# GpSimd stops scaling queries in batch 4, and its residual adds are laid out apart from VectorE's two-input operations

## The chip, the cores and the metric

The kernel runs on one core of one Trainium2 chip. The metric is the device time of one execution in microseconds. The median of three runs of the kernel before is 551.96 us (551.89 to 552.12).

## The reference

The input is attention data of 8 batches, 12 heads, 448 positions and a head dimension of 64, a mixing pair U, V of rank 32, and two channel matrices of 768 x 3072 and 3072 x 768. Cut to what matters:

```python
q_n = q / (norm(q) + 1e-6);  k_n = k / (norm(k) + 1e-6)
attn = softmax(q_n @ k_n.T / tau)            # per batch and head
x = (attn @ v), heads side by side           # 8 x 448 x 768
u = x + (x.T @ U @ V).T                      # mixes along the positions
out = u + relu(u @ w_ch1) @ w_ch2            # 8 x 448 x 768, float32
```

So each query and key is divided by its length, attention follows, then a low-rank mixing along the sequence with a residual, then a two-layer channel network with a residual.

## The kernel before, in words

**Tiling.** The 12 heads of a batch are 6 pairs. Queries and keys are loaded by GpSimd's DMA queue (L588), four heads at a time, as tiles of 112 partitions (`qk_all`). For each such group `squares` makes the squares (L636 on ScalarE, L640 on VectorE, L638 on GpSimd in one group of batch 0), L644 on VectorE sums them by head, L658 and L659 on ScalarE take the root by a logarithm and an exponential, and L664 and L666 on VectorE make the inverse. Then `norm` multiplies queries and keys by it, one operation of 112 x 512 elements for a pair of heads (L712): these are the unit vectors. SyncE's queue transposes each pair's unit vectors with a DMA (L728) into `sqk`. TensorE makes the scores in bursts of three tiles (L774, six or eight matmuls), ScalarE takes their exponential (L792), TensorE multiplies by the values (L819, 32 matmuls for a pair of heads), and VectorE divides by the row sums (L850 and L851), which also frees the PSUM banks of that product. The mixing is done by L934 (with U), a copy (L1439 on ScalarE or L1441 on VectorE), L987 (with V) and the residual add L996. The result goes through device memory (L1025) and comes back transposed (L884) and plain (L888).

**The channel network.** It runs over the 28 tiles of 128 rows: three tiles, one tile, and then 12 units of two tiles. A unit uses seven block products where plain blocking uses eight. In the first six of these units, the half-way units, only the second layer is done so: the first layer is L1263 with its relu in L1273 (ScalarE) or L1275 (VectorE), the sums of blocks that the seven products need are L1235, L1236, L1237 and L1246 on VectorE, and the products are L1292. ScalarE copies the first product out of PSUM (L1315), GpSimd makes three residual adds from that copy and the rows of u (L1317, 128 x 384 elements of float32 each, both inputs in SBUF), and VectorE adds the further products to them (L1310). The other six units do the first layer by seven products as well (L1156 on TensorE, L1178, L1184 and L1193 beside it), after sums of the weights (L1115 to L1118). `mlp_seven` makes both kinds; its argument `up` is None in a half-way unit.

**What sets the order.** Every operation is entered in a `Plan` with an engine, an assumed duration, what it depends on, the ring slots that it takes and frees, and a priority. `Plan.run` walks through assumed time and writes the instructions of each engine in the order in which it started them; on the chip each engine follows its order and waits on semaphores. TensorE and GpSimd have streams that keep their own order; VectorE, ScalarE and SyncE choose by priority among what is ready. An operation entered with `port=True` on VectorE isn't started in the plan while one of GpSimd's with `port=True` runs, and the reverse:

```python
def shared(o, e, r):
    return max(r, port["POOL" if e == "DVE" else "DVE"]) if o.port and e in port else r
```

On VectorE that holds for L640, L712, L1235 to L1237, L1246 and the sums of weights and columns. On GpSimd it holds for L638 and for L712. The chip has no such rule from the plan: there only the order and the semaphores count. While attention of the later batches goes on, the half-way units fill TensorE between bursts of scores and value products, all in one order.

`POOL_XN` gives, by batch, which of queries (0) and keys (1) have their L712 on GpSimd. Before the change that is batch 4's queries: six instructions, one for each pair.

Of the kernel before, what the change touches and what calls it, by code (L numbers as in the profile page):

```python
# [317 lines left out]
def kernel(  # L318
# [21 lines left out]
    CH = C // 2  # L340
# [7 lines left out]
    BURST = [1] + [2] + [3] * 6  # L348
    PLAIN = [3, 1]
    HALF = 6  # L350
    POOL_XN = {4: (0,)}
    WHOLE = 3
    LAST = {0: 0, 2: 2, 4: 4}
    WIDE = 1
# [155 lines left out]
    pool_y = plan.stream("POOL")  # L510
# [11 lines left out]
    def dve_t(n, fast=1, fixed=0.065):  # L522
        return fixed + n * 0.00105 / fast
# [176 lines left out]
    def norm(b, p, ld, la, inv, a, deps, pr, loaded):  # L700
# [6 lines left out]
        def part(i):  # L707
            def fn():
# [3 lines left out]
                (nc.gpsimd if pool_ else nc.vector).tensor_mul(dst, src, sc)  # L712
            pool_ = i in POOL_XN.get(b, ())
            return plan.add(Op("POOL" if pool_ else "DVE", 1.05 if pool_ else dve_t(512), fn, deps=[deps[i]], acq=[xn],
# [383 lines left out]
    def seven_rows(after, free):  # L1098

        A_ = w1_sb.rearrange("p (i e) (j g x) -> p i e j g x", e=2, g=2, x=128)  # L1100
        N = HF * 128
        homes = [X_t[:, 0:N], X_t[:, N:2 * N], qk_t[:, 1152:1152 + N],
                 v0[:, 0:N], qk_t[:, 3 * QC + 1024:3 * QC + 1024 + N], v0[:, N:2 * N]] + [
            attn_all[:, N * n:N * (n + 1)] for n in range(3)]
        homes = [x.rearrange("p (j x) -> p j x", x=128) for x in homes]
        S1, S2, S4 = homes[0:3], homes[3:6], homes[6:9]
        by = {}

        def rows_(f, deps, prio=2.5, eng="DVE"):
            e = nc.gpsimd if eng == "POOL" else nc.vector  # L1110
            return plan.add(Op(eng, N * 0.00203 if eng == "POOL" else 0.15 + N * 0.00053, lambda: f(e), deps=deps, prio=prio,
                               port=True), pool_s if eng == "POOL" else None)
        for i in (2, 0, 1):
            A11, A12, A21, A22 = A_[:, i, 0, :, 0], A_[:, i, 1, :, 0], A_[:, i, 0, :, 1], A_[:, i, 1, :, 1]
            a = rows_(lambda v, o=S1[i], x=A21, y=A22: v.tensor_add(o, x, y), free[i])  # L1115
            c = rows_(lambda v, o=S2[i], x=S1[i], y=A11: v.tensor_sub(o, x, y), [a, *free[3 + i]])
            d = rows_(lambda v, o=S4[i], x=A12, y=S2[i]: v.tensor_sub(o, x, y), [c, *free[6]], 3, "POOL" if i in () else "DVE")
            e = rows_(lambda v, o=A21, x=A11, y=A21: v.tensor_sub(o, x, y), [a, *after], 2.7)  # L1118
            by[i] = {3: d, 5: a, 6: c, 7: e}
        left = {1: lambda i, j: A_[:, i, 0, j, 0], 2: lambda i, j: A_[:, i, 1, j, 0], 3: lambda i, j: S4[i][:, j],  # L1120
                4: lambda i, j: A_[:, i, 1, j, 1], 5: lambda i, j: S1[i][:, j], 6: lambda i, j: S2[i][:, j],
                7: lambda i, j: A_[:, i, 0, j, 1]}
        return left, by
# [127 lines left out]
    def mlp_seven(tiles, right, made_by, up=None, after=()):  # L1251
# [4 lines left out]
        if up is None:  # L1256
            us, uT, ut = columns_of(tiles)
            rs = {}
            for j in range(HF):
                mm = Slot(r_up, 1)  # L1260
                for e in range(2):
                    for cc in range(CC):
                        o = plan.add(Op("PE", pe_t(256), lambda j=j, e=e, cc=cc, mm=mm: nc.tensor.matmul(  # L1263
                            out=mm.tile[:, 256 * e:256 * e + 256], lhsT=w1_sb[:, cc, (2 * j + e) * 128:(2 * j + e + 1) * 128],
                            rhs=uT.tile[:, cc, :], start=(cc == 0), stop=(cc == CC - 1)),
                            deps=ut if cc == 0 else [], acq=[mm] if cc == 0 and e == 0 else [], rel=[uT.slot]), pe_mlp)
# [36 lines left out]
        s1, y12, y22, y21, o11 = Slot(r_o, 3), *[Slot(r_o, 0) for _ in range(4)]  # L1303
# [8 lines left out]
        def tile_of(s):  # L1312
            return lambda: s.tile
        p1 = product(1, a, True, False)
        cp = plan.add(Op("ACT", 0.42, lambda: nc.scalar.copy(out=s1.tile, in_=a.tile[:, 0:CH]),  # L1315
                         deps=[p1, *after], acq=[s1], prio=-0.5))
        y = [plan.add(Op("POOL", 1.0, lambda y_=y_, u=u, c0=c0: nc.gpsimd.tensor_add(  # L1317
            out=y_.tile, in0=s1.tile, in1=u.tile[:, c0:c0 + CH]), deps=[cp, u.back], acq=[y_], rel=[s1, u]), pool_y)
            for y_, u, c0 in ((y12, u1, CH), (y22, u2, CH), (y21, u2, 0))]
        if up is not None:  # L1320
            d = Slot(r_mm4, 1)
# [188 lines left out]
    def att(b):  # L1510
# [17 lines left out]
        out=lead.tile[:, i], in_=src[0, 0:2].rearrange("h (s c) d -> s h (c d)", c=SC)),  # L1528
        acq=[uv], prio=-5, lat=2.5)) for i, src in enumerate((q, k))]
# [8 lines left out]
    for c in range(SC):  # L1538
# [8 lines left out]
                        deps=[zf, *begun], prio=-2, lat=12.0))]  # L1547
# [45 lines left out]
    for n in range(0, len(rest), 2):  # L1593
        if n // 2 == HALF:
            up = seven_rows([hosts[-1][0][-1]], [
                [o for t in range(4) for o in made[3, t][:1]]] * 2 + [
                [o for p in range(NPAIR) for o in got[B - 1, p, "qkT"][1]] if i in (2, 4) else
                [last_av[B - 1 if i == 6 else B - 2, p] for p in range(NPAIR)] for i in range(2, 7)])
            held = stores + [last_av[B - 1, p] for p in range(NPAIR)]
            up = *up, [o for p in range(NPAIR) for o in got[B - 1, p, "qkT"][1]], [last_av[B - 1, p] for p in range(NPAIR)], bursts[B - 1][-1:]  # L1600
        hosts.append(mlp_seven(rest[n:n + 2], *seven, *((up, held) if n // 2 >= HALF else ())))
# [52 lines left out]
```

## Time and profile before

| | |
|---|---|
| median of the runs | 551.96 us |
| profiled execution | 551.44 us |
| its span, first to last instruction | 549.4 us |
| TensorE, matmuls | 539.7 us busy, 98% |
| VectorE | 447.4 us, 81% |
| ScalarE | 284.8 us, 52% |
| GpSimd | 149.6 us, 27% |
| granted TensorE clock | 1.0 |

GpSimd's busy time holds its DMA issues (some 0.7 us each) as well as its arithmetic. How to read rows of the profile: a row of a timeline gives the start and the duration in us, the engine (PE is TensorE, PEld its weight loads, DVE VectorE, ACT ScalarE, POOL GpSimd), the line, the operation, its output and input by name, and how many instructions are merged; the bracket at the end is idle time before it and what ended that. A row of the waits says who waited for whom: us in total, how often, the longest. A row of groups gives a count, then busy us and mean ns of one, then idle us in front of the group and what ended them. A row of the table by stages gives the stage, its length, and the busy us of PE, PEld, DVE, ACT and POOL with the numbers of instructions, then clock, DMA share and GB/s.

### The profile page before, as it was taken

The page shows a single profiled execution, that of the slowest core. Times are in us where ns is not written, and L with a number is a line of the kernel's source. Part 1 is how long each engine was busy: PE and PEld are TensorE (multiplying, and loading weights), DVE is VectorE, ACT ScalarE, POOL GpSimd, SP SyncE. Part 2 cuts the span into 40 slices and gives each one's busy share as a digit, 9 for nine tenths or more (in the row PEclk, how much of TensorE's full clock was granted, in tenths as well). Part 3 has the DMA queues.
Part 4 walks back from the last instruction along what each step waited for, and adds up shares of the span by engine and source line. Part 5 has one row for each costly group of instructions (what it writes and reads, how often), then busy time and mean ns, then how long its engine had stood idle before and what let it go on. Part 6 is the DMA issues. An engine that isn't in the chain of part 4 may idle for free.

```text
span 549.4 us, 15010 instructions
## 1 busy us (share of the span) xinstructions
PE 539.7 (98%) x6199; PEld 389.9 (71%) x6199; DVE 447.4 (81%) x1020; ACT 284.8 (52%) x466; POOL 149.6 (27%) x186
## 2 busy tenths in 40 slices
PE   8899999999999999999999999999999999999996
PEld 6565556677757657767857856778778787878783
DVE  8979969999797888979889896687978585858583
ACT  7976646566566765865765854642313141414140
POOL 8636233100624641511621620020201111111111
PEclk9999999999999999999999999999999999999999
DMA  9999999941998987996997994112141212121301
GB/s 154 202 208 138 205 204 153 225 73 43 145 183 125 109 151 91 156 159 110 134 155 123 106 139 102 38 32 87 30 137 30 88 30 88 31 87 30 88 2 57
DMA packets 142324, 61.09 MB, mean 111 GB/s; under 512 B 101008, under 2 KB 142256, under 8 KB 142256
## 3 DMA queue, kind: packets, MB, share of 16 engines
q0 software_dynamic: 72352, 25.73, 44.6%
q1 hardware_dynamic: 69904, 34.41, 29.6%
q8 instruction: 48, 0.79, 0.6%
q14 instruction: 20, 0.16, 0.1%
HBM read 56.93 MB, written 15.93 MB: 133 GB/s over the span
## 4 chain that ended last, share of the span: by engine, by line
PE 92%; DVE 5%; ACT 1%; POOL 1%; DMA 1%; issue 0%; DVEq 0%; POOLq 0%
PE bank L1292 30%; PE bank L1263 17%; PE bank L1156 15%; PE bank L819 8%; PE bank L774 7%; PE bank L1375 6%; PE bank L1417 6%; PE bank L987 2%; DVE qk_all L712 1%; DVE ss L644 1%; PE bank L934 1%; POOL sqk L638 1%; DMA relu<-in_q_dram 1%; PE bank L566 1%; DVE relu L1236 0%
## 5 line engine op out<-in xcount | busy, mean ns | idle before, releaser
L792 ACT ACTIVATE attn<-bank 128x896 bf16<-128x896 f32 (+1 forms) x163 | 140.2, 916 | 33.4 <-PE bank L774 32.8
L1292 PEld LDWEIGHTS <-relu 128*128 128x128 bf16 x1008 | 96.0, 98 | 66.1 <-issue 6.2
L1263 PE MATMUL bank<-uT,w_sb 128*128 128x256 bf16 x864 | 103.7, 273 | 0.0
L1292 PE MATMUL bank<-w_sb,relu 128*128 128x384 bf16 x576 | 102.6, 326 | 0.0
L1263 PEld LDWEIGHTS <-w_sb 128*128 128x128 bf16 x864 | 81.8, 98 | 17.7 <-issue 7.1
L644 DVE TENSOR_REDUCE ss<-sqk 112x8 f32<-112x512 bf16 x96 | 62.5, 675 | 2.3 <-ACT sqk L636 1.8
L819 PEld LDWEIGHTS <-attn 128*128 128x128 bf16 (+1 forms) x1536 | 54.0, 97 | 6.5 <-issue 3.2
L819 PE MATMUL bank<-v_nat,attn 128*128 128x65 bf16 (+1 forms) x1536 | 57.1, 193 | 0.8 <-DVE X_sb L857 0.7
L1273 ACT ACTIVATE relu<-bank 128x512 bf16<-128x512 f32 x56 | 33.4, 596 | 45.8 <-PE bank L1263 42.8
L712 DVE TENSOR_TENSOR qk_all<-qk_all,inv 112x512 bf16<-112x512 bf16 x87 | 56.6, 683 | 0.2
L588 POOL DMA_DIRECT2D qk_all<-in_q_dram x24 | 17.6, 733 | 138.2 <-ACT relu L1273 63.4
L774 PE MATMUL bank<-sqk 64*128 64x448 bf16 (+1 forms) x384 | 49.0, 358 | 1.9 <-DVE X_sb L851 1.1
L1156 PEld LDWEIGHTS <-w_sb 128*128 128x128 bf16 x864 | 49.2, 98 | 0.8
L1193 ACT COPY attn<-bank 128x512 f32<-128x512 f32 x18 | 10.4, 586 | 73.7 <-PE bank L1156 72.8
L1156 PE MATMUL bank<-uT,w_sb 128*128 128x128 bf16 x648 | 38.1, 219 | 0.0
L1184 ACT ACTIVATE relu<-relu 128x512 bf16<-128x512 bf16 x36 | 22.7, 630 | 29.8 <-DVE relu L1178 28.9
L611 POOL DMA_DIRECT2D v_nat<-in_v_dram x42 | 31.0, 748 | 16.8 <-DMA w_sb<-in_moe_w_ch_dram 12.8
L636 ACT ACTIVATE sqk<-qk_all 112x512 bf16<-112x512 bf16 x47 | 28.5, 630 | 13.4 <-DVE ss L644 13.3
L1375 PE MATMUL bank<-uT,w_sb 128*128 128x384 bf16 (+1 forms) x288 | 35.4, 273 | 0.0
L1417 PE MATMUL bank<-w_sb,relu 128*128 128x384 bf16 x192 | 35.3, 326 | 0.0
L851 DVE TENSOR_TENSOR X_sb<-bank,rd 128x256 bf16<-128x256 f32 x72 | 30.6, 425 | 2.5
L774 PEld LDWEIGHTS <-sqk 64*128 64x128 bf16 (+1 forms) x384 | 13.0, 96 | 26.5 <-issue 22.3
(134 smaller groups left out, 823.6 us busy)
## 6 DMA issues: line engine op xcount, KB each, us to landing
qk_all<-in_q_dram POOLq DMA_DIRECT2D x23, 224.0 KB, 5.1
qk_all<-in_k_dram POOLq DMA_DIRECT2D x23, 224.0 KB, 6.5
u_nat<-u SPq DMA_DIRECT2D x25, 192.0 KB, 2.9
w_sb<-in_moe_w_ch_dram POOLq DMA_DIRECT2D x4, 1152.0 KB, 18.4
w_sb<-in_moe_w_ch_dram POOLq DMA_DIRECT2D x8, 576.0 KB, 15.6
u<-X_sb SPq DMA_DIRECT2D x22, 192.0 KB, 2.4
v_nat<-in_v_dram POOLq DMA_DIRECT2D x11, 168.0 KB, 8.8
out_dram<-O_sb SPq DMA_DIRECT2D x11, 168.0 KB, 2.7
```

The source lines that it names most:

```text
L611: ops = [load(lambda j=j, r0=r0, c=c, s0=s0, s1=s1: nc.gpsimd.dma_start(out=v_t[b % 2][r0:r0 + s1 - s0, :, j, 0:D], in_=src[c, s0:s1]), (s ...
L644: lambda i=i, a0=a0, a1=a1, sq=sq: nc.vector.reduce_sum(ss.tile[:, i, a0:a1, :].rearrange("p h c -> p (h c)"), sq.tile[:, 0:a1 - a0, :].re ...
L712: (nc.gpsimd if pool_ else nc.vector).tensor_mul(dst, src, sc)
L774: nc.tensor.matmul(out=out, lhsT=qkT.tile.rearrange("p b s -> p (b s)")[r, n0:n0 + w], rhs=qkT.tile[r, SC:2 * SC, :].rearrange("p c s -> p ...
L792: exps.append(plan.add(Op("ACT", act_t(2 * S, 0.08), lambda sc=sc, c=c, attn=attn: nc.scalar.activation(out=attn.tile[:, :, off:off + S] i ...
L819: nc.tensor.matmul(out=av.tile[:, t, 0:D + 1], lhsT=tail.tile[:, hh, 128 * t:128 * (t + 1)] if tail and j == SC - 1 else (attn if j < SC - ...
L1156: o = plan.add(Op("PE", pe_t(128), lambda i=i, j=j, jj=jj: nc.tensor.matmul(out=mm.tile[:, 128 * jj:128 * jj + 128], lhsT=left[k](i, j), r ...
L1263: o = plan.add(Op("PE", pe_t(256), lambda j=j, e=e, cc=cc, mm=mm: nc.tensor.matmul(out=mm.tile[:, 256 * e:256 * e + 256], lhsT=w1_sb[:, cc ...
L1273: nc.scalar.activation(out=dst, in_=mm.tile[:, 0:512], func=AF.Relu)
L1292: o = plan.add(Op("PE", pe_t(CH), lambda j=j: nc.tensor.matmul(out=mm.tile[:, 0:CH], lhsT=left[k](j), rhs=right[k](j), start=(first and j ...
L1375: o = plan.add(Op("PE", pe_t(n), lambda cc=cc: nc.tensor.matmul(out=mm.tile[:, m:m + n], lhsT=w1_sb[:, cc, f * 128:(f + 1) * 128], rhs=uT. ...
L1417: nc.tensor.matmul(out=mm.tile[:, 0:c1 - c0], lhsT=relu.tile[:, f, i * 128:(i + 1) * 128], rhs=w2_t[:, f, c0:c1], start=(f == 0), stop=(f ...
```

## The change

Batch 4's six L712 of the queries go from GpSimd to VectorE. And the residual adds of the half-way units (18 of L1317) are entered with `port=True`, so that the plan lays them out apart from VectorE's operations that carry the same mark; in the other six units they stay as they were. No computation changes. The order of every engine changes from about 171 us on (VectorE first, TensorE from the burst of scores at 187.67 us), up to the first L1156 of the seventh unit; behind it TensorE's order is the same again.

```diff
@@ -348,7 +348,7 @@
     HALF = 6
-    POOL_XN = {4: (0,)}
+    POOL_XN = {}
     WHOLE = 3
@@ -1315,7 +1315,7 @@
         y = [plan.add(Op("POOL", 1.0, lambda y_=y_, u=u, c0=c0: nc.gpsimd.tensor_add(
-            out=y_.tile, in0=s1.tile, in1=u.tile[:, c0:c0 + CH]), deps=[cp, u.back], acq=[y_], rel=[s1, u]), pool_y)
+            out=y_.tile, in0=s1.tile, in1=u.tile[:, c0:c0 + CH]), deps=[cp, u.back], acq=[y_], rel=[s1, u], port=up is None), pool_y)
             for y_, u, c0 in ((y12, u1, CH), (y22, u2, CH), (y21, u2, 0))]
```

## The prediction

> **What bounds the kernel now.** I read the page's first part, then TensorE's waits, then the timelines of all engines around each place where TensorE was late. First the page: the span and the busy times.
>
> ```profile
> span 549.4 us, 15010 instructions
> PE 539.7 (98%) x6199; PEld 389.9 (71%) x6199; DVE 447.4 (81%) x1020; ACT 284.8 (52%) x466; POOL 149.6 (27%) x186
> ```
>
> TensorE works in 539.7 of 549.4 us and sets the time. The table by stages puts some 8 of the 9.7 idle us into the first and last 50 us, before the change begins and behind its last instruction. So two questions decide: which of the waits in between go, and which come. The matrix products are the same in number and shape. TensorE's own waits, and below them the stage in which the edited units lie (busy us of each engine, instructions, granted clock, DMA share, GB/s):
>
> ```profile
> PE bank L774 <- DVE X_sb L851: 1.1, 1, 1.1
> PE bank L987 <- ACT attn L792: 0.2, 1, 0.2
> ```
> ```profile
> 150.00:200.00 50.00, 48.89 (x493) 33.15 (x492) 41.93 (x93) 33.02 (x52) 23.28 (x29) 1.00 1.02 142
> ```
>
> From 150 to 335 us these are the only two waits. To find waits too short for a view I added up steps (start of one block of matmuls to the start of the next: L1263 0.109 us a matmul, L1292 0.163, L819 0.0305, a burst of L774 0.68 for six and 0.80 for eight, and 0.09 more in front of each burst). From 140 to 352 us only two blocks exceed their sum by over 0.1 us: one at 183.45 us, by 1.19, and one at 325.62, by 0.62. Nearly all other time there is TensorE at its pace. The timeline of the first place:
>
> ```profile
> 184.19 2.60 DVE L1236 TENSOR_TENSOR relu<-relu 128x384 bf16<-128x384 bf16 x1
> 184.52 2.05 POOL L712 TENSOR_TENSOR qk_all<-qk_all,inv 112x512 bf16<-112x512 bf16 x2
> 187.19 0.42 DVE L851 TENSOR_TENSOR X_sb<-bank,rd 128x256 bf16<-128x256 f32 x1
> 187.67 0.74 PE L774 MATMUL bank<-sqk 64*128 64x448 bf16 x6 [1.11 <-DVE X_sb L851]
> ```
>
> VectorE's L1236 takes 0.35 us elsewhere; here it lasts as long as GpSimd's two L712 and 0.2 more. Queued behind it is L851, which frees the PSUM bank that the next burst of scores needs; TensorE stands for 1.1 us. The second place:
>
> ```profile
> 320.33 0.90 POOL L1317 TENSOR_TENSOR relu<-relu,u_nat 128x384 f32<-128x384 f32 x1 [4.57 <-ACT relu L1315]
> 320.41 2.16 DVE L640 TENSOR_TENSOR sqk<-qk_all 112x512 bf16<-112x512 bf16 x2
> 321.21 2.13 POOL L1317 TENSOR_TENSOR O_sb<-relu,u_nat 128x384 f32<-128x384 f32 x2
> 324.26 0.23 ACT L658 ACTIVATE ln<-ss 112x32 f32<-112x32 f32 x1 [2.38 <-DVE ss L644]
> 324.66 2.51 ACT L792 ACTIVATE attn<-bank 128x896 bf16<-128x896 f32 x3
> 325.62 1.44 PE L819 MATMUL bank<-v_nat,attn 128*128 128x65 bf16 x32
> 327.22 0.32 PE L987 MATMUL bank<-A_sb,V_sb 128*128 128x384 bf16 x1 [0.16 <-ACT attn L792]
> ```
>
> Here GpSimd's residual adds hold up L640: two of them take 0.75 us at 277.46, 2.16 here. L644 is late, ScalarE stands in its queue at L658, the exponentials L792 behind it are late, and the value product L819 waits for them: 0.62 us. Both losses have one cause, the one that the two edits speak of.
>
> **Part one: no L712 on GpSimd.** The groups of GpSimd and VectorE:
>
> ```profile
> L712 POOL TENSOR_TENSOR qk_all<-qk_all,inv 112x512 bf16<-112x512 bf16 x6 | 6.7, 1129 | 7.9 <-DMA out_dram<-O_sb 4.5 <-DVE inv L666 3.4
> ```
> ```profile
> L712 DVE TENSOR_TENSOR qk_all<-qk_all,inv 112x512 bf16<-112x512 bf16 x87 | 56.6, 683 | 0.2
> ```
>
> GpSimd loses six instructions, 6.7 us. VectorE gains six at 0.605 us (the step of three in a row, 1.89 us with the last one's 0.68): 3.6 us. It gets back 2.25 at L1236 (2.60 less 0.35) and 0.77 at 192.76 if the adds there miss the L640 (1.18 us for 0.41). In the stage 150 to 200 us VectorE's 41.93 busy us become 41.93 - 2.25 - 0.77 + 3.63 = 42.5 of 50: room is left.
>
> What of the 2.25 lay on the path is found by walking VectorE through its new order from 171.0 us, where the orders part, with the steps above and TensorE unchanged. One L712 fits into the gap before 171.95, when VectorE waited for a value product; L1275 waits for TensorE at 176.33 as before; then two L640, four L644, three L1275, L1235, L1236 and L1237 run between the same TensorE events, and the second L851 ends at about 185.0 us. The burst stands two L1263 earlier in TensorE's new order and would start at 186.3. The slack is 1.3 us, so the wait of 1.19 goes whole. I walked on to 195.5: GpSimd's first add can start at 190.6 instead of 191.88, L1310 then waits for TensorE alone, and the product that needs it comes at 195.5. No new wait appears.
>
> A rule of the Trainium skill (SBUF — State Buffer, "Who interferes with whom") prices this differently: an operation of VectorE with two inputs in SBUF and a GpSimd operation that reads SBUF lock each other out for a whole instruction. By it, all three pairs of L712 cost VectorE up to 6.7 us. By the rows only one did: at 169.49 VectorE read PSUM (L850, L851 at their usual 0.17 and 0.42), at 198.08 it was GpSimd that waited (2.55 us for 2.05). By the rule the sum would be 6.7 - 3.6 = 3.1 us of VectorE won, by the rows 2.25 - 3.6 = 1.4 lost; I take the rows, and for TensorE the 1.19. The row goes beyond the rule in that L1236 was held through two instructions.
>
> The same section speaks against the edit: the six L712 remain two-input operations and can now be held by the adds. Loads that GpSimd issues are not slowed: six L611 beginning at 176.52 took 4.41 us, 0.735 each, while VectorE ran two L640. On GpSimd's queue the loads of batch 5 no longer stand behind L712, and SyncE's transposes of batch 4 leave with VectorE's L712; their bursts of scores stand many us later in TensorE's order, so both are costed at nothing. Without that cover a transpose behind a late L712 would cost what that is late, at most 0.6 us each.
>
> **Part two: the adds with `port`.** It changes no instruction; it changes where the order puts them and their neighbours. The first unit's adds (151.22) come before the orders part. At the fifth unit VectorE's new order has no L640 in front of the L1310 that wait for the first and second add; an L640 follows, where only the third add (0.87 us) can hold it. That delay is 0.54 less than the 1.41 of before (2.16 - 0.75), so 0.08 of the 0.62 would stay at most; I take 0.62 as gone.
>
> **What the new order costs.** Every burst after 187 us has moved by some matmuls. Two bounds. For a wait from load I summed VectorE's operations between value products, against TensorE's time: the tightest new stretches are 6.9 us of work against 6.6, and 7.6 against 7.5 (before: at most 8.8 against 10.6 in the long ones, 5.5 against 6.0). Below zero nothing can come, since TensorE's steps don't depend on the order; above, 0.3 and 0.1. The row nearest is the trace itself: 200 us in such an order with no wait but the two; I take 0.15.
>
> The other is the end of attention. The last value product stood 48 L1292 ahead of the first L1156, now 12 (2.0 us). With T the start of L1156, VectorE's last L851 ends at T - 1.1, then two L1117 (0.87 each) go before the L1310 that frees a bank, at T + 1.1 instead of T + 0.7. The 13th L1156 comes at T + 0.67, the 25th at T + 1.34: nothing if the 25th takes that bank, 0.5 if the 13th does. I take 0.2.
>
> **The sum.** 1.19 + 0.62 - 0.15 - 0.2 = 1.46 us. The profiled execution took 551.44 us, 549.4 of span and 2.0 around it; it becomes 550.0. The median shown, 551.96, is 0.52 above that execution, so it becomes **550.5 us**.
>
> **Rivals.** (1) *The lock only moves.* The exclusion exists in the layout alone; the chip still lets GpSimd start when its input comes. One of the four later triples of adds catches an L640, L712 or L1246 ahead of an L851, as at 192.76 (0.77 us) or at 320.41. For it: those two; against it: at 234.61 and 278.24 nothing reached TensorE. Time: 551.96 - 1.46 + 0.9 (between 0.62 and 1.19) = 551.4.
>
> (2) *VectorE becomes the bound of the units around batch 4*, and the result is slower. Place: the value products from 190 to 255 us, where the stretch holds 6.9 us of work for 6.6 and the adds' 2.65 us (0.91 and 1.77) may lie on a two-input operation. Each L851 that is late keeps a bank from the next burst, and the backlog passes on, since the stretch behind has no room. Price: 2.3 us of lock (as at L1236) plus 0.4 of overload, twice. It decides once the delay exceeds the slack of 1.3 us that the walk found: 2 x (2.7 - 1.3) = 2.8, which eats up the gain; a third such place makes 4.2. Time: 551.96 - 1.81 + 4.2 = 554.3. Against it: VectorE's 42.5 of 50.
>
> (3) *The edits do nothing for TensorE*: another chain ends at the same burst. Then 551.9. The walk speaks against it, so it shares the chance of (1).
>
> **How the numbers follow.** Forecast 0.52; (1) with (3) 0.30; (2) 0.18. A measurement of this kernel tells about 0.2% from no change: 1.1 us, so faster begins below 550.86 and slower above 553.06. Faster 0.52, same 0.30, slower 0.18. The likeliest case alone goes from 550.1 (both waits gone, none new) to 550.9. The range reaches down to 550.0 and up to 553.4, into (2) far enough to leave about 0.15 above and 0.05 below.
>
> **What would show it.** Right: no L712 on GpSimd; L1236 nowhere above 0.5 us near 184; no wait of TensorE for L851 there; L640 near the fifth unit's adds at 0.4 each; TensorE busy 539.7 in a span of 548. Wrong: new lines of TensorE's waits for L851, L1441 or L792 between 190 and 375 us, or a wait at the first L1156; VectorE's L640, L712 or L1246 lasting 1 to 3 us beside L1317.

## The result, and the profile after

The changed kernel takes 549.81 us (median of five, 549.14 to 549.98) against 551.89 us for the kernel before on the same occasion (551.51 to 552.12). The ratio is 0.9959, with a 95% interval of 0.9945 to 0.9974: faster by 2.1 us, where 1.46 was forecast. The time lies just below the range on record (550.0 to 553.4), so the forecast was right in direction and in cause and wrong in size. The profiled execution took 549.28 us.

The first part of the page, the change:

```profile
span 547.5 us, 15002 instructions
PE 538.8 (98%) x6199; PEld 389.0 (71%) x6199; DVE 449.0 (82%) x1029; ACT 284.2 (52%) x463; POOL 141.6 (26%) x180
```

GpSimd loses 8.0 us, VectorE gains 1.6, and the span is shorter by 1.9. TensorE's waits between 150 and 335 us, of which there were two before, are an empty list now. The table by stages (stage, length, busy us of PE, PEld, DVE, ACT and POOL, clock, DMA share, GB/s):

```profile
150.00:200.00 50.00, 50.00 (x527) 34.12 (x525) 44.04 (x102) 34.11 (x54) 16.94 (x23) 1.00 1.03 143
```

TensorE is busy in all 50 us where it was in 48.89; VectorE does 44.04 us of work instead of 41.93. The two places that the prediction showed, in the timelines after. First the burst of scores that had waited for L851:

```profile
184.05 0.35 DVE L1236 TENSOR_TENSOR relu<-relu 128x384 bf16<-128x384 bf16 x1
184.80 0.42 DVE L851 TENSOR_TENSOR X_sb<-bank,rd 128x256 bf16<-128x256 f32 x1
185.73 2.50 DVE L712 TENSOR_TENSOR qk_all<-qk_all,inv 112x512 bf16<-112x512 bf16 x4
186.18 0.74 PE L774 MATMUL bank<-sqk 64*128 64x448 bf16 x6
```

L1236 is back at 0.35 us, L851 ends at 185.22, and the burst starts on time at 186.18. Then the adds of the fifth unit:

```profile
318.05 0.93 POOL L1317 TENSOR_TENSOR relu<-relu,u_nat 128x384 f32<-128x384 f32 x1
318.93 1.79 POOL L1317 TENSOR_TENSOR O_sb<-relu,u_nat 128x384 f32<-128x384 f32 x2
319.06 0.42 DVE L851 TENSOR_TENSOR X_sb<-bank,rd 128x256 bf16<-128x256 f32 x1
319.95 0.55 DVE L1310 TENSOR_TENSOR relu<-bank,relu 128x384 f32<-128x384 f32 x1
320.88 0.68 DVE L712 TENSOR_TENSOR qk_all<-qk_all,inv 112x512 bf16<-112x512 bf16 x1
324.87 0.41 DVE L640 TENSOR_TENSOR sqk<-qk_all 112x512 bf16<-112x512 bf16 x1
```

While GpSimd adds, VectorE now runs L850, L851 and L1310, which read PSUM, all at their usual length; L712 begins after the adds, and L640 takes 0.41 us.

**A measure finer than the median.** The waits in question are 0.6 to 1.2 us, and the medians of one and the same kernel scatter by nearly as much: the kernel before has 551.40 to 551.97 us on the occasions of this study. I therefore read one stage from every profile: from the start of the L934 at about 144 us to the start of the first L1156. TensorE does the same matmuls in it in all kernels, only in another order; in the five profiles that have the change's order and no added work in this stage it takes 230.53 us each time. Before, it lasts 376.83 - 144.47 = 232.36 us; in the change 374.91 - 144.38 = 230.53, that is 1.83 less. The two waits on record were 1.19 + 0.62 = 1.81. What comes before that L934 was 0.09 us shorter, and from the first L1156 to TensorE's end both take 168.3 us. So the difference of the spans, 1.92 us, is the two waits and these 0.09, and nothing was paid for the new order.

The times differ by more than the spans, 2.16 us for the two profiled executions. Each timed run has its span on record too. The time around the span is 1.94 to 2.08 us in all 84 such runs of the kernel before and 1.74 to 1.81 in the five of the change, so 0.23 us of the gain lie ahead of the first instruction or behind the last. Of the 2.08 us between the medians, 1.83 + 0.23 = 2.06 are thus accounted for.

### The profile page after: what moved, and what is told of

The parts are those of the page before. It is cut to its first block, busy times and chain, and to the rows that moved or that the text cites. A ratio compares the mean times of both kernels' runs of the same rounds, so it can differ in the third digit from the quotient of the medians.

```text
span 547.5 us, 15002 instructions
## 1 busy us (share of the span) xinstructions
PE 538.8 (98%) x6199; PEld 389.0 (71%) x6199; DVE 449.0 (82%) x1029; ACT 284.2 (52%) x463; POOL 141.6 (26%) x180
## 4 chain that ended last, share of the span: by engine, by line
PE 94%; DVE 3%; ACT 1%; POOL 1%; DMA 1%; issue 0%; DVEq 0%; POOLq 0%
PE bank L1292 30%; PE bank L1263 18%; PE bank L1156 15%; PE bank L819 8%; PE bank L774 7%; PE bank L1375 6%; PE bank L1417 6%; PE bank L987 2%; DVE qk_all L712 1%; PE bank L934 1%; DVE ss L644 1%; POOL sqk L638 1%; PE bank L566 1%; DMA relu<-in_q_dram 1%; DVE X_sb L857 0%; ACT attn L787 0%
## 5 line engine op out<-in xcount | busy, mean ns | idle before, releaser
L712 DVE TENSOR_TENSOR qk_all<-qk_all,inv 112x512 bf16<-112x512 bf16 x93 | 60.3, 683 | 0.3
L819 PEld LDWEIGHTS <-attn 128*128 128x128 bf16 (+1 forms) x1536 | 54.0, 97 | 6.5 <-issue 2.9
L819 PE MATMUL bank<-v_nat,attn 128*128 128x65 bf16 (+1 forms) x1536 | 57.1, 193 | 0.6 <-DVE X_sb L857 0.6
L1273 ACT ACTIVATE relu<-bank 128x512 bf16<-128x512 f32 x47 | 28.1, 597 | 45.7 <-PE bank L1263 45.5
L1156 PEld LDWEIGHTS <-w_sb 128*128 128x128 bf16 x864 | 49.3, 98 | 0.8
L1156 PE MATMUL bank<-uT,w_sb 128*128 128x128 bf16 x648 | 38.1, 219 | 0.0
L636 ACT ACTIVATE sqk<-qk_all 112x512 bf16<-112x512 bf16 x54 | 32.8, 632 | 10.0 <-DVE ss L644 9.5
L851 DVE TENSOR_TENSOR X_sb<-bank,rd 128x256 bf16<-128x256 f32 x72 | 30.6, 425 | 2.5
```

The costliest lines, as they stand in the source:

```text
L636: nc.scalar.activation(out=y, in_=x, func=AF.Square)
L819: nc.tensor.matmul(out=av.tile[:, t, 0:D + 1], lhsT=tail.tile[:, hh, 128 * t:128 * (t + 1)] if tail and j == SC - 1 else (attn if j < SC - ...
L1156: o = plan.add(Op("PE", pe_t(128), lambda i=i, j=j, jj=jj: nc.tensor.matmul(out=mm.tile[:, 128 * jj:128 * jj + 128], lhsT=left[k](i, j), r ...
```

## The experiments

**Each part alone.** The first kernel has only the first edit, the second only the second.

```diff
# e1_queries_only
-    POOL_XN = {4: (0,)}
+    POOL_XN = {}
```


> Part one alone: no L712 on GpSimd, the adds not marked. Theory (the lock between GpSimd's arithmetic and VectorE's two-input operations is the only cause of both waits): the wait of 1.19 us near 184 us is gone, the adds can still catch a two-input operation, so 0 to 0.8 us of such a wait stays; 549.9 to 550.9 us. Rival (the gain comes from the new order as such, not from the lock): anywhere, waits of TensorE would stand where no two-input operation of VectorE is held.

```diff
# e2_adds_only
-            ... rel=[s1, u]), pool_y)
+            ... rel=[s1, u], port=up is None), pool_y)
```


> Part two alone: the adds of the half-way units marked, batch 4's six L712 of the queries still on GpSimd. Theory of the lock: the wait at the fifth unit (0.62 us) goes; GpSimd's L712 were marked already and still collide on the chip, so a wait of 0 to 1.2 us stays near 175 to 205 us; 550.0 to 551.4 us. Rival (the order): about as fast as both parts together, 549.8.

Measured, with 551.62 us for the kernel before beside them: the queries alone 550.68 us, ratio 0.998 (0.9973 to 0.9987), stage 230.84 us; the adds alone 550.95 us, ratio 0.999 (0.9983 to 0.9996), stage 231.42. With the queries alone the wait at 184 us is gone, and a new one of 0.31 us stands at the fifth unit, by the same cause with other instructions (timeline of that kernel):

```profile
320.07 2.23 POOL L1317 TENSOR_TENSOR O_sb<-relu,u_nat 128x384 f32<-128x384 f32 x2
320.61 2.24 DVE L712 TENSOR_TENSOR qk_all<-qk_all,inv 112x512 bf16<-112x512 bf16 x2
322.98 0.42 DVE L851 TENSOR_TENSOR X_sb<-bank,rd 128x256 bf16<-128x256 f32 x1
323.49 1.05 PE L774 MATMUL bank<-sqk 64*128 64x448 bf16 x6
323.52 0.42 DVE L851 TENSOR_TENSOR X_sb<-bank,rd 128x256 bf16<-128x256 f32 x1
```

Two L712, 1.28 us elsewhere, take 2.24 beside the adds; the two L851 behind them are late. The second ends at 323.94, in the midst of the burst, which stands there until 324.00 and takes 1.05 us, 0.74 elsewhere. That is rival (1) of the prediction, in the kernel that lacks the second edit. With the adds alone the wait at the fifth unit is gone and the first one stays, at 0.89 us by the stage (231.42 - 230.53):

```profile
184.88 2.35 DVE L1236 TENSOR_TENSOR relu<-relu 128x384 bf16<-128x384 bf16 x1
184.94 2.06 POOL L712 TENSOR_TENSOR qk_all<-qk_all,inv 112x512 bf16<-112x512 bf16 x2
188.10 0.74 PE L774 MATMUL bank<-sqk 64*128 64x448 bf16 x6 [0.85 <-DVE X_sb L851]
```

Each edit removes its own wait, and in the order that it makes the other place loses less than before (0.31 for 0.62 us, 0.89 for 1.19); both are needed for the sum. The medians of single kernels are coarser than the stages: these two lie 0.94 and 0.67 us below the kernel before, the two that follow 1.10 and 0.60, where the stages are shorter by 1.52, 0.94, 1.17 and 0.93.

**Lock or order.** Both edits also change the order of every engine, so the gain could be the order's. To tell the two apart, one kernel keeps the old order and issues GpSimd's scaling on VectorE:

```diff
# e3_old_order_no_pool_scaling: the plan still places it as GpSimd's
-                (nc.gpsimd if pool_ else nc.vector).tensor_mul(dst, src, sc)
+                nc.vector.tensor_mul(dst, src, sc)
```


> The order of before is kept, only batch 4's six L712 of the queries are issued on VectorE at the place in the order where GpSimd had them. Theory of the lock: L1236 near 184 us at 0.35, no TensorE wait there, the 0.62 us near 325 us stays: 551.9 - 1.2 = 550.7. Rival (the new order makes the gain): VectorE only gets 3.6 us more work in an order that didn't count on it, TensorE waits for L851 as before or longer, 551.9 to 553.

Measured: 550.52 us, ratio 0.9978 (0.9969 to 0.9987), stage 231.19 us. That is 1.17 less than before, the wait at 184 us and nothing else; the 0.62 us are still there. Timeline of the first place:

```profile
184.05 0.35 DVE L1236 TENSOR_TENSOR relu<-relu 128x384 bf16<-128x384 bf16 x1
184.79 0.42 DVE L851 TENSOR_TENSOR X_sb<-bank,rd 128x256 bf16<-128x256 f32 x1
186.35 0.74 PE L774 MATMUL bank<-sqk 64*128 64x448 bf16 x6
```

Another keeps the old order and takes the reading out of the adds:

```diff
# e4_adds_as_memset
-            Op("POOL", 1.0, lambda ...: nc.gpsimd.tensor_add(out=y_.tile, ...
+            Op("POOL", 1.0, lambda ...: nc.gpsimd.memset(y_.tile, 0.0) if up is None else nc.gpsimd.tensor_add(out=y_.tile, ...
```


> Before, with the 18 residual adds of the half-way units replaced by a GpSimd memset of the same tile (the residual and the first product are left out there), so that GpSimd reads nothing from SBUF in them. Theory of the lock: two L640 near 320 us at 0.75 together, TensorE's 0.62 us near 325 us gone, the 1.19 us near 184 us stays: 551.9 - 0.6 = 551.3. Rival (GpSimd's writes hold VectorE too, or ScalarE's queue is late for another reason): the 0.62 stays, 551.9.

Measured: 551.02 us, ratio 0.9988 (0.9982 to 0.9995), stage 231.43 us. The 0.62 us are gone and 0.89 of the 1.19 stay. At the fifth unit:

```profile
320.73 0.76 DVE L640 TENSOR_TENSOR sqk<-qk_all 112x512 bf16<-112x512 bf16 x2
323.23 0.23 ACT L658 ACTIVATE ln<-ss 112x32 f32<-112x32 f32 x1 [1.08 <-DVE ss L644]
325.95 1.14 PE L819 MATMUL bank<-v_nat,attn 128*128 128x65 bf16 x32
```

L640 takes 0.76 us for two, ScalarE's wait at L658 falls from 2.38 to 1.08, and L819 has its usual length (1.14 us; 1.44 before). One limit: a memset waits for no copy from ScalarE, so here it had run at 314.65 already; this shows that the adds caused the delay, not yet that writing alone is harmless. Another place of the same kernel bears on that:

```profile
190.41 0.44 POOL L1317 MEMSET relu<- 128x384 f32 x1
190.56 0.36 DVE L1236 TENSOR_TENSOR relu<-relu 128x384 bf16<-128x384 bf16 x1
190.77 0.80 POOL L1317 MEMSET O_sb<- 128x384 f32 x2
190.84 0.35 DVE L1237 TENSOR_TENSOR relu<-relu 128x384 bf16<-128x384 bf16 x1
```

L1236 and L1237 run inside GpSimd's memsets and lose nothing. The two L640 behind them, the operation that was held at the fifth unit, begin at 191.11 and 191.44 beside the third memset (191.13 to 191.56) and keep 0.42 us each.

Then both changes of these two kernels together, still in the old order, with the change beside it:

> The order of before, with both sources of the lock taken out: batch 4's six L712 of the queries issued on VectorE in the old place, and the 18 adds of the half-way units a memset (residual and first product left out there). Theory of the lock: the stage from the L934 at 144 us to the first L1156 takes 232.36 - 1.19 - 0.62 = 230.55 us, the same as in the change (230.53), so the new order gives nothing of its own. Rival (the new order is worth something itself): it stays above 230.8.

> The change once more, beside the run in front of it on the same chip: the same stage of 230.5 us. If the surplus of the medians over the sum of the two waits (2.08 against 1.81 us) is scatter of the first 145 us, the profile's L934 comes anywhere from 144.3 to 145.3 us and the ratio to before lies between 0.996 and 0.998.

Measured, with 551.97 us for the kernel before beside them: the old order without the lock 549.73 us, ratio 0.9959 (0.9944 to 0.9974), stage 230.55 us; the change again 549.84 us, ratio 0.996 (0.9946 to 0.9974), stage 230.53. Neither has a wait of TensorE between 130 us and the end. The old order reaches the new one's stage to 0.02 us, as the sum 232.36 - 1.19 - 0.62 says. In the stage the new order gives nothing beyond the two waits; it is the means to keep the operations apart. The rival falls, with one reserve for the second wait: a memset is also shorter than an add (0.44 us for 0.91) and waits for no copy from ScalarE, so it is not the reading alone that this kernel takes out there.

**The lock put back into the new order.**

```diff
# e5_new_order_pool_scaling: the plan still places it as VectorE's
-                (nc.gpsimd if pool_ else nc.vector).tensor_mul(dst, src, sc)
+                (nc.gpsimd if b == 4 and i == 0 else nc.vector).tensor_mul(dst, src, sc)
```


> The order of the change is kept, only batch 4's six L712 of the queries are issued on GpSimd at the place in the order where VectorE had them. Theory of the lock: GpSimd's L712 (1.03 us each) again meet two-input operations of VectorE, one of the three pairs costs VectorE 1 to 2.5 us, and TensorE waits 0 to 1.2 us where an L851 stands behind it: 549.8 to 551.0, with every new TensorE wait behind a lengthened operation. Rival (the order): no wait, 549.8.

Measured: 550.13 us beside 551.40 for the kernel before, ratio 0.997 (0.9961 to 0.998), stage 230.53 us and no wait of TensorE between 130 us and the end. The operations do meet, in the timeline:

```profile
185.32 0.42 DVE L851 TENSOR_TENSOR X_sb<-bank,rd 128x256 bf16<-128x256 f32 x1
186.26 2.14 DVE L712 TENSOR_TENSOR qk_all<-qk_all,inv 112x512 bf16<-112x512 bf16 x2
186.31 2.99 POOL L712 TENSOR_TENSOR qk_all<-qk_all,inv 112x512 bf16<-112x512 bf16 x2 [1.90 <-DVE inv L666]
186.94 0.74 PE L774 MATMUL bank<-sqk 64*128 64x448 bf16 x6
```

VectorE's two L712 take 2.14 us instead of 1.28 and GpSimd's two 2.99 instead of 2.05. But L851 stands in front of them here, not behind. So this lock costs nothing; in the places above it cost where something that TensorE needs was queued behind the held operation. The theory's expectation left this open (0 to 1.2 us); taken as a proof of the lock this run gives nothing.

**The two charges of the sum.** I had charged 0.2 us for the hand-over to the first L1156 and 0.15 for VectorE's load. Two kernels lengthen VectorE's work ahead of the L1310 that frees the last bank:

```diff
# e6_one_more_before_last_add (n = 2), e6_three_more_before_last_add (n = 4)
-            d = rows_(lambda v, o=S4[i], x=A12, y=S2[i]: v.tensor_sub(o, x, y), ...
+            d = rows_(lambda v, o=S4[i], x=A12, y=S2[i], n=2 if i == 2 else 1: [v.tensor_sub(o, x, y) for _ in range(n)], ...
```


> The change, with the first of the three L1117 done twice: 0.87 us more of VectorE ahead of the L1310 that frees the last bank of the half-way units at the first L1156. If my walk of the hand-over was right in place and the bank is wanted by the 25th L1156 (slack 0.2 us): TensorE waits 0.6 to 0.7 us there. If the bank is wanted later still (slack over 0.9): no wait, and the 0.2 us that I charged was nowhere near.

> The same with the first L1117 done four times, 2.6 us more. With a slack of 0.2 us: a wait of 2.4. With a slack of 0.9 to 1.5: a wait of 1.1 to 1.7. No wait at all: the hand-over doesn't hang on that L1310.

In the change itself, with T = 374.91 the start of L1156:

```profile
373.85 1.82 DVE L1117 TENSOR_TENSOR attn<-w_sb,v_nat 128x1536 bf16<-128x1536 bf16 x2
374.91 2.17 PE L1156 MATMUL bank<-uT,w_sb 128*128 128x128 bf16 x36
375.58 0.55 DVE L1310 TENSOR_TENSOR relu<-bank,relu 128x384 f32<-128x384 f32 x1
376.92 0.22 PE L1156 MATMUL bank<-qk_all,v_nat 128*128 128x128 bf16 x1
```

L1310 starts at T + 0.67 and ends at T + 1.22; the walk had it free the bank at T + 1.1. With three more L1117:

```profile
378.65 0.55 DVE L1310 TENSOR_TENSOR relu<-bank,relu 128x384 f32<-128x384 f32 x1
379.26 0.22 PE L1156 MATMUL bank<-qk_all,v_nat 128*128 128x128 bf16 x1 [2.08 <-DVE relu L1310]
```

The matmul that waits is the first after the 36, the 37th, wanted at T + 2.01; I had considered the 13th and the 25th. It starts 0.06 us after L1310 ends. In the change L1310 ends at 376.13, so the slack is 376.92 - 376.13 - 0.06 = 0.73 us. The lengthened kernels agree: one more L1117 moves L1310 from T + 0.67 to T + 1.67, and the 37th starts 0.26 us late; three more move it to T + 3.65, by 2.98, and it starts 2.25 late (2.98 - 0.73). Neither kernel came out as I expected: a slack of 0.73 us lies between the cases that I had set down. Their single times are 550.16 and 552.51 us.

The second of them loses another 0.86 us further on, in a later unit whose adds are not marked. There three of VectorE's sums of blocks take some 1.13 us each instead of 0.42 while GpSimd adds, and TensorE waits for one of them:

```profile
451.31 3.01 POOL L1317 TENSOR_TENSOR O_sb<-relu,u_nat 128x384 f32<-128x384 f32 x3 [23.41 <-ACT relu L1315]
453.48 1.13 DVE L1236 TENSOR_TENSOR relu<-relu 128x512 bf16<-128x512 bf16 x1
454.66 0.82 PE L1292 MATMUL bank<-uT,relu 128*128 128x384 bf16 x4 [0.70 <-DVE relu L1236]
```

In the change the sums at this place keep 0.42 us, and GpSimd's three adds take longer:

```profile
448.97 4.32 POOL L1317 TENSOR_TENSOR O_sb<-relu,u_nat 128x384 f32<-128x384 f32 x3 [23.40 <-ACT relu L1315]
```

So the same operations meet in both kernels, and which engine is held differs.

The load:

```diff
# e7_more_load
-            (nc.gpsimd if pool_ else nc.vector).tensor_mul(dst, src, sc)
+            [nc.vector.tensor_mul(dst, src, sc) for _ in range(2 if b == 4 and i == 1 else 1)]
```


> The change, with batch 4's six L712 of the keys done twice: 3.6 us more VectorE work between 171 and 205 us, three times what I charged as overload there would need. If VectorE was near its limit in that stage, as the charge of 0.15 us supposed: TensorE waits for L851 by 1 us or more in sum. If the slack in front of the bursts (1.3 us by the walk) takes it: 0 to 0.5 us.

Measured: one time of 551.44 us, stage 231.75, which is 1.22 above the change. The rows of the six added L712 come to 4.15 us (3.6 expected), so some 30% of the work is felt; by size that is the first of the two cases. The waits are not where I expected them: not for L851 but for relus of the first layer (the kernel's waits):

```profile
PE bank L1292 <- DVE relu L1275: 0.4, 1, 0.4
PE bank L1263 <- DVE relu L1275: 0.4, 1, 0.4
```

The first stands at 191.09 us, for a relu that was ScalarE's (L1273) in the kernel before; the second only at 217.58, well behind the added work. VectorE is not far from its limit there: 2.9 us of 4.15 were absorbed. The 0.3 and 0.1 us of overload that I had counted were absorbed as well: the change has no wait there, and its stage no loss.

## Why the prediction was wrong in size and right in cause

**Right: both waits and their cause.** L1236 near 184 us at 0.35, L851's end at 185.2 (walked: 185.0), the burst on time; L640 at 0.41 beside the adds; 1.83 us for 1.81. The runs confirm the chain, not only the coincidence: taking GpSimd's two-input work away in the old order takes away exactly these waits.

**The terms that failed: "What the new order costs", 0.15 + 0.2.** Both measured 0. The walk to L1310 was right to about 0.1 us (T + 1.22 for T + 1.1), but which matmul takes its bank was left as a guess between the 13th and the 25th; it is the 37th, with 0.73 us to spare. The charge for load took the excess of a stretch's work over TensorE's time as if no slack lay in front of it, although the walk had just found 1.3 us there. Without the two charges the sum is 551.96 - 1.81 = 550.15.

**The term that was carried over: the 2.0 us around the span.** The sum put them into the new time unchanged, without a reason. They measured 1.78, and 551.96 - 1.81 - 0.23 = 549.92. The kernel before was also 0.07 us lower on the occasion of the result (551.89), which gives 549.85; measured are 549.81. That this closes so well is in part luck. In the profiles the L934 at the stage's start comes anywhere from 144.33 to 145.29 us, with the order before it unchanged, so a median of a few runs can lie some tenths off.

The time around the span goes with what GpSimd does and not with the order. It is 1.94 to 2.08 us in the kernels in which GpSimd has both the six L712 and the 18 half-way adds (the kernel before, the adds alone, the L712 put back), and 1.72 to 1.84 in all others, those in the old order too. What makes the difference stays open.

**The range's lower end, 550.0.** It left 0.15 us below 550.15, less than the 0.23 of the term held fixed, and less than the scatter of the medians that it was made from.

**Wrong, and harmless by luck: VectorE's 42.5 us.** It is 44.0. The new order also redistributes work that either engine may do, which the sum left out: in this stage VectorE has six L1275 instead of four, 1.4 us more (in the whole kernel 25 instead of 16, and 36 L640 instead of 43). It did not matter for the time, but a load of 42.5 was part of the case against rival (2).

**The rivals.** (1), a lock that only moves, happened in the kernel with the first edit alone (0.31 us) and not in the change: there an add holds no operation of VectorE between 165 and 355 us. (2), VectorE as the bound, needs more than the 4.15 us of rows added in e7_more_load to eat up the gain: they took 1.22 of 1.83. (3), another chain that ends at the same burst, is refuted by the change and by e3_old_order_no_pool_scaling: the wait at 184 us goes whole.

**The rule of the skill.** By the Trainium skill (SBUF — State Buffer, "Who interferes with whom") all three pairs of L712 lock, and the prediction's estimate from that was up to 6.7 us of VectorE's time; the row said 2.25, and TensorE gained 1.17. The rule tells which operations hold each other, the trace which of them mattered. Its exception for GpSimd operations that only write agrees with the memsets: L1236 and L1237 at 0.36 and 0.35 us inside them.

## What to carry to other kernels

When VectorE and GpSimd both do two-input work in SBUF, look for operations of either that last a multiple of their usual time, and price only those with something behind them that the bound engine needs and that comes later than its slack allows. An order that is written out by a plan can be tested apart from its contents: keep the plan's placement and change only what is issued there. A charge for "the new order" has to name the instruction that would wait; if it can be walked to 0.1 us, it can also be walked to the matmul that takes the bank. And a term that is carried over unchanged, as the time around the span here, is a term of the forecast too: it needs its own scatter.

## What the runs showed of the hardware that I had not expected

- VectorE can be held through two GpSimd instructions in a row: L1236 for 2.60, 2.35 and 2.30 us beside two L712 of 2.05 together, in three kernels (before, the adds alone, the adds as memset). Elsewhere it got in between: at 320.41 us its two L640 took 1.11 and 1.13 us beside three adds, and in the new order with the L712 put back VectorE's and GpSimd's L712 took turns (186.26 to 189.30 us). What decides between the two is not shown.
- GpSimd can be the one that is held: two L712 in 2.55 and 2.99 us instead of 2.05, three adds in 4.32 instead of 2.65. The start in the row does not tell who: VectorE's L712 at 198.03 began 0.05 us ahead of GpSimd's and kept its 0.69 us; L1236 at 184.19 began 0.33 ahead and was held to the end of both.
- An operation on one tensor from SBUF in float32 can be held as well: L664 took 0.93 us at 236.37 in the kernel before, beside an add of 0.90, and 0.17 elsewhere.
- Memsets on GpSimd held nothing: beside them L1236, L1237 and L640 kept 0.36, 0.35 and 0.42 us.
- TensorE takes a freed bank 0.06 us after the end of the VectorE operation that frees it (L851 to 187.61, the burst at 187.67; L1310 to 379.20, the matmul at 379.26).
